# f64 weights by byte planes: two word shifts and a sign step replaced by two bf16 products

## The chip, the cores and the metric

The kernel runs on one core of a Trainium2 chip. Its engines are TensorE (PE: matmul; PEld: its weight loads), VectorE (DVE), ScalarE (ACT), GpSimd (POOL) and SyncE (SP), each with an instruction stream of its own that it works through in order; 16 DMA engines move data between HBM and SBUF. The metric is the device time of one execution, in microseconds; the median of 3 runs counts. Line numbers of the profile (L368) are lines of the kernel file. Nearly all of the first phase has the line L368, because a recorder collects the instructions and issues them from that line in an order that it plans; there the names of the tiles tell instructions apart.

## The reference

Three stages are computed, one after another:

```python
S_re, S_im = a*S (complex) + k x v          # gated recurrence over 768 steps, 4 x 8 heads of 48
y[:, :, t] = einsum(q[:, :, t], S_re)       # attention output
x = y as 3072 tokens x 384
h = max(x @ w1, x @ w2, x @ w3)             # 384 -> 768; the three weights and w_out are float64
x = (h @ w_out)                             # 768 -> 384
expert = argmax(softmax(cos(x, emb) / tau)) # one of 8 experts for each token
out = gate * (relu(x @ W1[e]) @ W2[e])      # 384 -> 1024 -> 384, float32 weights
```

The weights `w1`, `w2`, `w3` and `w_out` come as 8-byte floats. The host passes their bytes on as they are; the kernel makes float32 of them. This conversion is what the change is about.

## The kernel before

Phase 1 works on 12 units of 256 time steps (3 units for each of 4 batches). For each unit DVE and ACT prepare the complex decay (`front`: normalise; `mid`: running products; `back`: products with q and k into the tile `QK`), a DMA lays `QK` out by heads into a tile `S`, and TensorE does the attention of the unit's two halves (`attn`: transposes `pk`, scores `pa`, masked by DVE into `at`, state `pT`, output `py`), then the first MoE layer (`moe1`: products `ph` with `w1` and `w3`, maximum on DVE, products `px` with `w_out`). Float32 products are made of halves: a tile `xhi` that TensorE takes in one pass and a remainder `xlo`, and the same for weights (`whi`, `wlo`). Phase 2 sorts tokens by expert and runs the experts; its instructions stand in program order and are untouched by the change.

`weights` runs once, at the start of phase 1, and its products are needed by the first `ph`. It goes through 24 tiles of 128 x 384 f64 numbers: 6 of `w2` transposed (`w2t`), 12 of `w1` and `w3` (`w123`, loaded to tiles `r`), 6 of `w_out` (`wo`). POOL issues one DMA for each. Before the change a tile is converted so: ACT scales the upper word, read as float32, by 2^-112 (`f`), which shifts its exponent; the sign is set apart (for three tiles in four by two ACT instructions, Sign and a scaled Copy, for the fourth by one DVE mask); DVE shifts `f` left by 3 and puts the sign in, and a second DVE instruction shifts the lower word right by 29 and puts it in. A `w123` tile then goes on to TensorE: two passes with the identity bring it to a PSUM tile `pd`, products with `minus` subtract the `w2t` part, ACT copies `pd` out as `w` hi, TensorE subtracts that, ACT copies the rest out as lo. A `wo` tile is transposed (`pwt`), copied (`wt`) and multiplied with the expert embedding (`pG`); when all six are there, DVE copies `pG` into `wo`, and TensorE makes `pw` of `wo` and `w2t`. `pd`, `pwt`, `pw` and `ph` share three PSUM buffers with the tag "h".

The order of the instructions is made by a planner (`Recorder`): a list schedule with costs for each instruction, run forward and backward, in which each instruction has a key (unit number plus an offset of its stage) and a small bias by its kind (table `BIAS`). Where the plan leaves TensorE idle, `keep_warm` puts in short products with the identity (line 627). The order on each engine is fixed at build time; at run time an engine waits for semaphores.

Of the kernel before, what the change touches and what calls it, by code (L numbers as in the profile page):

```python
# [12 lines left out]
I32 = mybir.dt.int32  # L13
U32 = mybir.dt.uint32
# [109 lines left out]
class Recorder:  # L124
# [88 lines left out]
    def access(self, op, ap, write):  # L213
# [10 lines left out]
        else:  # L224
            idx = np.array([f])
# [3 lines left out]
            bits = np.zeros(pitch, np.uint8)  # L229
# [98 lines left out]
    def issue(self):  # L328
# [30 lines left out]
        for i in seq:  # L359
# [12 lines left out]
    BIAS = {"Cts": -0.91, "Cv": 0.78, "Gs": -0.3, "QKrv": -1.34, "QKs": -0.19, "Sg": 1.22, "Ss": 0.13, "Xg": 1.31,  # L372
            "Xs": -0.15, "cvhs": -1.13, "embv": -0.21, "enTv": -1.28, "end_s": -0.07, "fms": 1.79, "hhi_s": 0.15,
            "hlo_v": -0.8, "nrmss": 0.99, "nrmsv": -1.69, "pa_t": -0.95, "posv": 0.62, "pwtt": -1.99, "px__s": -1.23,
            "px__t": 0.63, "pyt": -0.99, "scv": 0.33, "w_s": 0.43, "wts": 1.11, "xhis": -1.08}
# [7 lines left out]
class Prog:  # L383
# [6 lines left out]
    def consts(self, pool):  # L390
# [22 lines left out]
        self.tiny = pool.tile([128, 1], F32, name="tiny")  # L413
        nc.gpsimd.memset(self.tiny, 1e-38)
# [294 lines left out]
    def weights(self, split=True):  # L709
# [45 lines left out]
        for k, (src, m, i, c) in enumerate(todo):  # L755
# [6 lines left out]
            raw = raw.rearrange("p (n w) -> p n w", w=2)  # L762
            f, sg = hs[k % 5], part(7 + k % 3).bitcast(I32)
            h = f.bitcast(I32)
            with self.keyed(-4 + k * 0.01):
                if split and k == self.AHEAD[0]:
                    self.load_a(1, q.gpsimd)
                if split and k == self.AHEAD[1]:
                    self.load_qk(0, q.gpsimd)
                q.gpsimd.dma_start(raw, src.bitcast(I32).rearrange("p (n w) -> p n w", w=2))  # L770
            if split and k % self.SIGNS:

                s.activation(sg.bitcast(F32), raw[:, :, 1].bitcast(F32), AF.Sign, bias=self.tiny)
                s.activation(sg, sg.bitcast(F32), AF.Copy, scale=2.0 ** 30, bias=-2.0 ** 30)
            else:
                v.tensor_scalar(sg, raw[:, :, 1], -0x80000000, None, op0=ALU.bitwise_and)
            s.activation(f, raw[:, :, 1].bitcast(F32), AF.Copy, scale=2.0 ** -112)
            v.scalar_tensor_tensor(h, h, 3, sg, op0=ALU.logical_shift_left, op1=ALU.bitwise_or)
            o = self.wo[:, i, :DM] if m is None else f if split and c is not None else w2t[:, i] if split else \
                self.w[:, m, i, c:c + n]  # L780
            v.scalar_tensor_tensor(o.bitcast(I32), raw[:, :, 0], 29, h, op0=ALU.logical_shift_right, op1=ALU.bitwise_or)
            if split and c is not None:
                both = self.tl(self.mw, [128, 2, n], f"w{m}{i}{c}", 1, f"w_{m}{i}{c}", F32R)
                self.whi[m, i, c // n], self.wlo[m, i, c // n] = both[:, 0], both[:, 1]
                pd = self.tl(self.pf, [128, n], "h", 3, f"pd{k}")
# [366 lines left out]
    SIGNS = 4  # L1152
# [634 lines left out]
```

## Time and profile before

| | |
|---|---|
| median of 3 runs | 778.13 us (777.83 to 778.33) |
| the profiled execution | 777.83 us, its span 775.9 us |
| TensorE busy | 719.6 us, 93% of the span |
| VectorE busy | 607.1 us, 78% |
| ScalarE busy | 441.5 us, 57% |
| mean granted TensorE clock | 0.983 of full speed |

The span is what the trace covers; 1.9 us of the execution lie outside it. Phase 1 reaches to about 513 us, phase 2 from there to the end. A busy time of an instruction includes its start-up, which overlaps with the one before it on the same engine; the distance of two starts is what an instruction costs in a full stream. In the names, numbers of buffers are left out.

### The profile page before, as it was taken

Reading aid. Unit: us, or ns where it says so; the run is one execution under the profiler, and the core shown is the slowest. Engines: PE = TensorE matmul, PEld = TensorE weight load, DVE = VectorE, ACT = ScalarE, POOL = GpSimd, SP = SyncE. Lnnn points to the kernel's source line nnn. Section 1 sums busy time; section 2 is a strip of 40 time slices with the busy share of each in tenths; the row PEclk is TensorE's granted clock in tenths of the full one; section 3 lists DMA queues with packets and bytes.
Section 4 is the critical chain, followed back from the end, with each engine's and each line's share of the span. In section 5 each row is a group of like instructions: output and inputs, shape, how many; then the busy total and the mean of one; then the engine's idle time right before and its main releaser. Section 6 shows DMA issues by size and latency. Waiting matters only on the chain. (4 is left out here: it accounts for less than half of the span.)

```text
span 775.9 us, 18425 instructions
## 1 busy us (share of the span) xinstructions
PE 719.6 (93%) x7318; PEld 657.1 (85%) x7318; DVE 607.1 (78%) x1211; ACT 441.5 (57%) x1007; POOL 104.6 (13%) x156
## 2 busy tenths in 40 slices
PE   0568989999999999999999999999999999999995
PEld 0447679899899989888998988989989898999985
DVE  8999799999999999999999722869986455546420
ACT  8997485656667555757455442167535466544521
POOL 6301000000000000000000000022122223324211
PEclk9987899999999999999999999999999999999999
DMA  8608062635345380834516240051058775691500
GB/s 330 263 21 197 1 174 69 139 131 137 106 105 119 91 209 13 197 99 119 137 37 140 60 86 22 13 233 42 22 236 335 283 299 213 210 368 49 186 22 26
DMA packets 28753, 107.42 MB, mean 138 GB/s; under 512 B 5061, under 2 KB 8180, under 8 KB 25569
## 3 DMA queue, kind: packets, MB, share of 16 engines
q1 hardware_dynamic: 20432, 77.55, 33.5%
q0 software_dynamic: 7952, 28.21, 11.3%
q8 instruction: 59, 0.97, 0.5%
q10 hardware_dynamic: 272, 0.39, 0.1%
q14 instruction: 38, 0.30, 0.1%
HBM read 96.35 MB, written 10.62 MB: 138 GB/s over the span
## 5 line engine op out<-in xcount | busy, mean ns | idle before, releaser
L368 PE MATMUL ph<-xhi,w 128*128 128x256 f32 x864 | 134.0, 291 | 0.9 <-ACT xhi L368 0.9
L368 PEld LDWEIGHTS ph<-xhi,w 128*128 128x128 f32 x864 | 114.3, 191 | 8.3 <-issue 4.7
L1298 DVE TENSOR_TENSOR w2l<-queue_q_buf,w2h 128x768 fp32r<-128x768 f32 x52 | 47.9, 954 | 39.1 <-ACT w2h L1297 39.0
L1336 PE MATMUL ph<-xh,w1s 128*128 128x256 f32 x264 | 77.0, 292 | 0.0
L368 PE MATMUL ph<-xlo,w 128*128 128x256 f32 x432 | 75.3, 283 | 0.4 <-DVE xlo L368 0.4
L1336 PE MATMUL ph<-xh,w1l 128*128 128x256 f32 x264 | 74.6, 283 | 0.0
L1336 PE MATMUL ph<-xl,w1s 128*128 128x256 f32 x264 | 74.6, 283 | 0.0
L1352 PE MATMUL py<-w2h,hlo 128*128 128x384 f32 x200 | 67.9, 340 | 1.8 <-DVE hlo L1341 1.8
L1352 PE MATMUL py<-w2h,hhi 128*128 128x384 f32 x200 | 69.1, 345 | 0.0
L1352 PE MATMUL py<-w2l,hhi 128*128 128x384 f32 x200 | 67.6, 338 | 0.0
L368 PEld LDWEIGHTS ph<-xlo,w 128*128 128x128 f32 x432 | 62.0, 191 | 0.6 <-DVE xlo L368 0.6
L368 POOL DMA_DIRECT2D v<-v x24 | 12.9, 538 | 365.4 <-PE py L368 364.5
L1341 DVE SCALAR_TENSOR_TENSOR hlo<-ph,hhi 128x512 fp32r<-128x512 f32 x50 | 34.3, 688 | 30.0 <-ACT hhi L1340 30.0
L1340 ACT ACTIVATE hhi<-ph 128x512 fp32r<-128x512 f32 x50 | 29.9, 598 | 49.0 <-PE ph L1336 48.8
L368 PE MATMUL pa<-S 112*128 112x128 f32 x384 | 51.7, 279 | 2.2 <-DVE at L368 1.7
L1336 PEld LDWEIGHTS ph<-xh,w1s 128*128 128x128 f32 x264 | 50.5, 191 | 3.8 <-issue 3.1
L368 PEld LDWEIGHTS pa<-S 112*128 112x128 f32 x384 | 48.2, 193 | 4.5 <-DVE at L368 2.9
L1297 ACT CAST w2h<-queue_q_buf 128x768 fp32r x52 | 40.8, 833 | 18.1 <-PE py L1352 16.7
L1336 PEld LDWEIGHTS ph<-xh,w1l 128*128 128x128 f32 x264 | 50.5, 191 | 0.5
L1336 PEld LDWEIGHTS ph<-xl,w1s 128*128 128x128 f32 x264 | 50.5, 191 | 0.0
L368 DVE TENSOR_TENSOR sa<-X 128x384 f32<-128x384 f32 x84 | 46.5, 554 | 0.7
L1292 DVE TENSOR_TENSOR w1l<-queue_q_buf,w1s 128x1536 fp32r<-128x1536 f32 x22 | 38.6, 1759 | 9.3 <-PE ph L1336 7.4
(399 smaller groups left out, 1809.1 us busy)
## 6 DMA issues: line engine op xcount, KB each, us to landing
queue_q_buf<-w SPq DMA_DIRECT2D x26, 1536.0 KB
S<-QK SPq DMA_DIRECT2D x46, 289.1 KB
X<-a SPq DMA_DIRECT2D x11, 768.0 KB
QKr<-qk SPq DMA_DIRECT2D x11, 768.0 KB
w1m<-w SPq DMA_DIRECT2D x5, 1536.0 KB
w2m<-w SPq DMA_DIRECT2D x5, 1536.0 KB
v<-v POOLq DMA_DIRECT2D x24, 224.0 KB, 3.6
r<-w POOLq DMA_DIRECT2D x12, 384.0 KB, 8.4
```

What stands on the lines that cost most here:

```text
L368: getattr(getattr(self.nc, c[0]), c[1])(*c[2], **c[3])
L1292: v.tensor_sub(wl[k], av.rearrange("p (a b) -> p a b", b=FF2)[:, :, c], w1[k].bitcast(F32))
L1297: s.copy(hi, b[:, c])
L1298: v.tensor_sub(lo, bv[:, c], hi.bitcast(F32))
L1336: t.matmul(ph[:, f], a, b, start=o == 0, stop=o == len(ops) - 1)
L1340: s.activation(hi, ph, AF.Relu).ins,
L1341: v.scalar_tensor_tensor(lo, ph, 0.0, hi.bitcast(F32), op0=ALU.max, op1=ALU.subtract).ins]
L1352: t.matmul(py, a[:, f, r], c[:, k % 4], start=o == 0, stop=o == 3 * KF - 1)
```

## The change

A double has its sign and the upper exponent bits in byte 7, and the rest of what a float32 needs in bytes 3 to 6. The new code loads the tile from byte 3 on (3069 bytes of each row of 3072, as bytes), so that bytes 3 to 6 of each number are one aligned word (`words`) and byte 7 is a small signed integer behind it (`top`). ACT makes relu(top + 72) as bf16, DVE makes top limited to -56..56 as bf16, and TensorE adds the first and subtracts the second in PSUM by two products with plus and minus identity (`sgn`, bf16): the sum is a small integer that holds sign and exponent. ACT scales it by 2^27, less a constant, into an integer word, and one DVE instruction shifts `words` right by 5 and puts that word in. For a `w123` tile the PSUM tile of these products is the `pd` that the later products use; the other tiles take one of the "h" buffers for it too. The sign by masks goes, with `SIGNS` and the constant `tiny`. The recorder's `access` now counts bytes in place of elements when it looks for overlaps, and the table `BIAS` has other values.

```diff
@@ -11,6 +11,7 @@
 F32R = mybir.dt.float32r
 BF16 = mybir.dt.bfloat16
 I32 = mybir.dt.int32
+I8 = mybir.dt.int8
 U32 = mybir.dt.uint32
 AF = mybir.ActivationFunctionType
 ALU = mybir.AluOpType
@@ -222,11 +223,12 @@
         elif ap.space == bass.MemoryType.DRAM:
             mask, p1 = -1, p0 + rows
         else:
-            idx = np.array([f])
+            idx, size = np.array([f]), mybir.dt.size(ap.dtype)
             for step, num in ap.ap[1:]:
                 if step:
                     idx = (idx[:, None] + step * np.arange(num)).reshape(-1)
-            bits = np.zeros(pitch, np.uint8)
+            idx = (idx[:, None] * size + np.arange(size)).reshape(-1)
+            bits = np.zeros(pitch * size, np.uint8)
             bits[idx] = 1
             mask, p1 = int.from_bytes(np.packbits(bits).tobytes(), "big"), p0 + rows
         new = (op, mask, p0, p1)
@@ -369,10 +371,8 @@
         return max(end)
 
     ENGINES = "vector", "scalar", "tensor", "gpsimd", "sync"
-    BIAS = {"Cts": -0.91, "Cv": 0.78, "Gs": -0.3, "QKrv": -1.34, "QKs": -0.19, "Sg": 1.22, "Ss": 0.13, "Xg": 1.31,
...
+    BIAS = {"M_s": -0.7, "QKv": 0.22, "Xg": -1.01, "Xv": -0.66, "enTv": -1.56, "fys": -0.19, "nrmsv": -0.29,
+            "rawxg": -1.19, "rg": 0.06, "sqxev": -0.1, "wtv": -0.72}
     PASSES, WAIT, LANES = 4, 130.0, 8
     START = {"vector": 1600.0, "gpsimd": 2200.0, "scalar": 2500.0, "sync": 1000.0}
     WINDOW = 4096 / 1.2
@@ -410,8 +410,11 @@
         idn = self.ident
         self.one = pool.tile([128, 1], F32, name="one")
         self.ln40 = pool.tile([128, 1], F32, name="ln40")
-        self.tiny = pool.tile([128, 1], F32, name="tiny")
-        nc.gpsimd.memset(self.tiny, 1e-38)
+        self.p72 = pool.tile([128, 1], F32, name="p72")
+        nc.gpsimd.memset(self.p72, 72.0)
+        self.sgn = pool.tile([128, 2, 128], BF16, name="sgn")
+        nc.scalar.copy(self.sgn[:, 0], self.ident)
+        nc.scalar.activation(self.sgn[:, 1], self.ident, AF.Copy, scale=-1.0)
         self.hln40 = pool.tile([128, 1], F32, name="hln40")
         nc.gpsimd.memset(self.one, 1.0)
         nc.gpsimd.memset(self.ln40, 40 * math.log(2))
@@ -759,30 +762,30 @@
             else:
                 raw = raws[ring if ring < 6 else 2 + ring % 4]
                 ring += 1
-            raw = raw.rearrange("p (n w) -> p n w", w=2)
+            row = raw.bitcast(I8)
+            words, top = raw[:, ::2], row[:, 4::8]
             f, sg = hs[k % 5], part(7 + k % 3).bitcast(I32)
-            h = f.bitcast(I32)
             with self.keyed(-4 + k * 0.01):
                 if split and k == self.AHEAD[0]:
                     self.load_a(1, q.gpsimd)
                 if split and k == self.AHEAD[1]:
                     self.load_qk(0, q.gpsimd)
-                q.gpsimd.dma_start(raw, src.bitcast(I32).rearrange("p (n w) -> p n w", w=2))
-            if split and k % self.SIGNS:
-
-                s.activation(sg.bitcast(F32), raw[:, :, 1].bitcast(F32), AF.Sign, bias=self.tiny)
-                s.activation(sg, sg.bitcast(F32), AF.Copy, scale=2.0 ** 30, bias=-2.0 ** 30)
-            else:
-                v.tensor_scalar(sg, raw[:, :, 1], -0x80000000, None, op0=ALU.bitwise_and)
-            s.activation(f, raw[:, :, 1].bitcast(F32), AF.Copy, scale=2.0 ** -112)
-            v.scalar_tensor_tensor(h, h, 3, sg, op0=ALU.logical_shift_left, op1=ALU.bitwise_or)
+                q.gpsimd.dma_start(row[:, :8 * n - 3], src.bitcast(I8)[:, 3:])
             o = self.wo[:, i, :DM] if m is None else f if split and c is not None else w2t[:, i] if split else \
                 self.w[:, m, i, c:c + n]
-            v.scalar_tensor_tensor(o.bitcast(I32), raw[:, :, 0], 29, h, op0=ALU.logical_shift_right, op1=ALU.bitwise_or)
+            both = f.bitcast(BF16)
+            up, mid = both[:, :n], both[:, n:]
+            s.activation(up, top, AF.Relu, bias=self.p72)
+            v.tensor_scalar(mid, top, -56.0, 56.0, op0=ALU.max, op1=ALU.min)
+            pd = self.tl(self.pf, [128, n], "h", 3, f"pd{k}")
+            with q.group() if split else ExitStack():
+                for x, j in ((up, 0), (mid, 1)):
+                    t.matmul(pd, self.sgn[:, j], x, start=j == 0, stop=j == 1)
+            s.activation(sg, pd, AF.Copy, scale=2.0 ** 27, bias=-72 * 2.0 ** 27)
+            v.scalar_tensor_tensor(o.bitcast(I32), words, 5, sg, op0=ALU.logical_shift_right, op1=ALU.bitwise_or)
             if split and c is not None:
                 both = self.tl(self.mw, [128, 2, n], f"w{m}{i}{c}", 1, f"w_{m}{i}{c}", F32R)
                 self.whi[m, i, c // n], self.wlo[m, i, c // n] = both[:, 0], both[:, 1]
-                pd = self.tl(self.pf, [128, n], "h", 3, f"pd{k}")
                 with q.group():
                     t.matmul(pd, self.ident, f, start=True, stop=True)
                     for b in range(3):
@@ -1149,7 +1152,6 @@
     SPLIT = 2
     BOTH = 1
     AHEAD = 3, 8
-    SIGNS = 4
     TAIL = 12000.0
     KEYS = {"conv": -0.9, "moe": 0.3, "mid": -1.0, "attn": -2.0, "back": -1.0, "front": -0.9, "early": 10.5, "max": 0.3}
```

The order changes on all engines. The numbers behind names are buffer numbers.

TensorE before, at its start: the first `w123` tiles go through `pd`; `cvh` and `S` hold the converted tile.

```order
L368 MATMUL pen<-ident,emb 128x8 x3
L627 MATMUL pd_169<-ident 128x128 x4
L368 MATMUL pd_169<-S_145,ident 128x384
L368 MATMUL pd_169<-minus,w2t 128x128 x3
L627 MATMUL pd_172<-ident 128x128 x2
L368 MATMUL pd_172<-S_145,ident 128x384
L368 MATMUL pd_172<-minus,w2t 128x128 x3
L368 MATMUL pd_176<-cvh_156,ident 128x384
L368 MATMUL pd_176<-minus,w2t 128x128 x3
L368 MATMUL pd_169<-w_168,minus 128x384
```

TensorE of the change, the first three `w123` tiles: the pair with `sgn` for the third of them, then the passes of all three.

```order
L370 MATMUL pd_184<-cvh_159,sgn 128x384
L370 LDWEIGHTS sgn
L370 MATMUL pd_184<-cvh_159,sgn 128x384
L370 MATMUL pd_177<-S_148,ident 128x384
L370 MATMUL pd_177<-minus,w2t 128x128 x3
L370 MATMUL pd_180<-S_148,ident 128x384
L370 MATMUL pd_180<-minus,w2t 128x128 x3
L370 MATMUL pd_184<-cvh_159,ident 128x384
L370 MATMUL pd_184<-minus,w2t 128x128 x3
L370 MATMUL pd_177<-w_178,minus 128x384
L370 MATMUL pd_180<-w_181,minus 128x384
L370 MATMUL pd_184<-w_185,minus 128x384
```

Each PSUM buffer is now taken two products earlier, and the tile passes ACT and DVE between the pair and the passes; TensorE's first instruction is no longer `pen` but such a pair for a `w2t` tile.

TensorE before, where the last `wo` tile has been turned: from the last `pG` to the third `pw`.

```order
L368 MATMUL pG<-enT,wt_216 128x8 x3
L368 MATMUL pa_1_254<-S_144 128x128 x4
L368 MATMUL pw_217<-wo,w2t 128x392 x6
L368 MATMUL pk_0_248<-ident,S_144 128x112 x4
L368 MATMUL pw_218<-wo,w2t 128x392 x6
L368 MATMUL pa_0_252<-S_144 128x128 x4
L368 MATMUL pk_0_261<-ident,S_144 128x112 x4
L368 MATMUL pw_219<-wo,w2t 128x392 x6
```

The same place of the change: `py_271` is the output of the first unit's first half.

```order
L370 MATMUL py_271<-xhi_273,unit 128x384
L370 MATMUL pG<-enT,wt_228 128x8
L370 MATMUL pG<-enT,wt_231 128x8 x3
L370 MATMUL pk_1_278<-ident,S_147 128x112 x4
L370 MATMUL pa_0_280<-S_147 128x128 x4
L370 MATMUL pa_1_282<-S_147 128x128 x4
L370 MATMUL pw_232<-wo,w2t 128x392 x6
```

The attention of the first unit's first half now stands ahead of the last `pG`; before it stood between and behind the `pw`.

DVE before, at the last masked scores (`at_1_337`) of the second unit.

```order
L368 SCALAR_TENSOR_TENSOR rr_380<-rr_380 128x768
L368 TENSOR_TENSOR at_0_335<-pa_0_334,mask 128x512
L368 TENSOR_TENSOR sb<-X_316 128x48
L368 TENSOR_TENSOR QK_381<-QKr_315,X_246 128x6x256
L368 TENSOR_TENSOR at_1_337<-pa_1_336,mask 128x512
L368 TENSOR_TENSOR Ct<-sb 128x24
```

DVE of the change at the same scores (`at_1_352`).

```order
L370 TENSOR_TENSOR at_0_350<-pa_0_349,mask 128x512
L370 TENSOR_TENSOR sa<-X_331 128x384
L370 SCALAR_TENSOR_TENSOR rr_395<-rr_395,QKr_330 128x768
L370 TENSOR_TENSOR X_331<-sa 128x2x96
L370 TENSOR_TENSOR QK_396<-rr_395,X_261 128x6x128
L370 TENSOR_TENSOR sa<-X_331 128x384
L370 TENSOR_TENSOR at_1_352<-pa_1_351,mask 128x512
```

Up to this row the change has 24 SCALAR_TENSOR_TENSOR of 128x384 fewer and 18 TENSOR_SCALAR of 128x384 more; of the third unit's preparation (`rr`, `QK`) more stands ahead of it, of the fourth unit's (`sa`, `X`) less.

## Rows read from the trace of the kernel before

**Rows 1.** The page: busy tenths of two engines in 40 slices of 19.4 us.
```profile
PE   0568989999999999999999999999999999999995
...
DVE  8999799999999999999999722869986455546420
```

**Rows 2.** Windows: busy us of each engine, TensorE's granted clock, DMA share, GB/s.
```profile
50.00:55.00 5.00, 2.16 (x13) 1.45 (x11) 5.00 (x10) 5.00 (x11) 0.00 (x0) 1.00 0.02 3
70.00:75.00 5.00, 4.81 (x23) 4.57 (x23) 4.90 (x18) 4.63 (x9) 0.04 (x1) 0.52 0.80 155
200.00:300.00 100.00, 99.27 (x1260) 91.38 (x1262) 96.72 (x193) 61.52 (x163) 2.68 (x5) 1.00 0.49 120
```

**Rows 3.** Waits of TensorE: who ended them, us in total, times, longest.
```profile
PE pen L368 <- DVE sb L368: 26.1, 1, 26.1
PE pd L368 <- ACT w L368: 9.4, 7, 2.1
```

**Rows 4.** Timeline of DVE: start, us, engine, line, operation, out<-in, shapes, [idle before].
```profile
31.63 0.54 DVE L368 SCALAR_TENSOR_TENSOR cvh<-r,cvh 128x384 int32<-128x384 int32 x1
32.10 0.23 DVE L368 TENSOR_TENSOR sb<-Ct,X 128x48 f32<-128x48 f32 x1
...
40.96 0.34 DVE L368 TENSOR_SCALAR S<-r 128x384 int32<-128x384 int32 x1
41.23 0.94 DVE L368 TENSOR_TENSOR m<-X,C 128x768 f32<-128x768 f32 x1
```

**Rows 5.** Timeline of ACT, 34 to 38 us.
```profile
34.13 0.53 ACT L368 ACTIVATE S<-S 128x384 int32<-128x384 f32 x1
34.54 0.56 ACT L368 ACTIVATE cvh<-r 128x384 f32<-128x384 f32 x1
35.00 0.55 ACT L368 ACTIVATE S<-r 128x384 f32<-128x384 f32 x1
...
36.62 0.84 ACT L368 CAST w<-pd 128x384 fp32r<-128x384 f32 x2
37.35 0.65 ACT L368 ACTIVATE S<-r,tiny 128x384 f32<-128x384 f32 x1
37.91 0.47 ACT L368 CAST w<-pd 128x384 fp32r<-128x384 f32 x1
```

**Rows 6.** Timeline of TensorE: weight and state products, the first MoE product, 384-column products.
```profile
92.06 4.13 PE L368 MATMUL pw<-wo,w2t 128*128 128x392 f32 x12
96.12 0.88 PE L368 MATMUL pT<-v,kt 128*32 128x48 f32 x64
...
107.17 0.97 PE L368 MATMUL ph<-xhi,w 128*128 128x256 f32 x6 [0.92 <-ACT xhi L368]
...
525.26 0.34 PE L1352 MATMUL py<-w2h,hlo 128*128 128x384 f32 x1
525.44 0.33 PE L1352 MATMUL py<-w2h,hhi 128*128 128x384 f32 x1
```

**Rows 7.** Timeline of DVE: idle times between 75 and 90 us.
```profile
79.45 0.21 DVE L368 COPY wo<-pG 128x48 f32<-128x48 f32 x1 [2.05 <-PE pG L368]
81.36 0.69 DVE L368 TENSOR_TENSOR at<-pa,mask 128x512 f32<-128x512 f32 x1 [0.53 <-PE pa L368]
87.76 0.96 DVE L368 TENSOR_TENSOR m<-X,C 128x768 f32<-128x768 f32 x1 [0.93 <-ACT C L368]
```

**Rows 8.** Timeline of DVE and TensorE: the second unit's last masked products.
```profile
137.08 0.68 DVE L368 TENSOR_TENSOR at<-pa,mask 128x512 f32<-128x512 f32 x1
...
135.16 2.80 PE L368 MATMUL px<-wo,h 128*128 128x392 f32 x8
...
139.47 1.05 PE L368 MATMUL py<-at,v 128*32 128x128 f32 x32
```

**Rows 9.** Timeline of POOL: two neighbouring loads of f64 weight tiles.
```profile
12.02 0.54 POOL L368 DMA_DIRECT2D r<-w  x1 [0.44 <-DMA r<-w]
12.99 0.54 POOL L368 DMA_DIRECT2D r<-w  x1 [0.44 <-DMA S<-w2t]
```

More of the change, by code (lines that the diff above doesn't have):

```diff
@@ L371 @@
     ENGINES = "vector", "scalar", "tensor", "gpsimd", "sync"
-    BIAS = {"Cts": -0.91, "Cv": 0.78, "Gs": -0.3, "QKrv": -1.34, "QKs": -0.19, "Sg": 1.22, "Ss": 0.13, "Xg": 1.31,
-            "Xs": -0.15, "cvhs": -1.13, "embv": -0.21, "enTv": -1.28, "end_s": -0.07, "fms": 1.79, "hhi_s": 0.15,
-            "hlo_v": -0.8, "nrmss": 0.99, "nrmsv": -1.69, "pa_t": -0.95, "posv": 0.62, "pwtt": -1.99, "px__s": -1.23,
-            "px__t": 0.63, "pyt": -0.99, "scv": 0.33, "w_s": 0.43, "wts": 1.11, "xhis": -1.08}
+    BIAS = {"M_s": -0.7, "QKv": 0.22, "Xg": -1.01, "Xv": -0.66, "enTv": -1.56, "fys": -0.19, "nrmsv": -0.29,
+            "rawxg": -1.19, "rg": 0.06, "sqxev": -0.1, "wtv": -0.72}
     PASSES, WAIT, LANES = 4, 130.0, 8
```

## The prediction

> **What bounds the kernel now.** I read the page's slices first. TensorE shows 9 in nearly every slice from the sixth on, and low digits in the first five; VectorE shows 9 up to the twenty-second [rows 1]. So the end is set by how early TensorE gets into its full stream. The windows say the same with numbers: from 200 to 300 us TensorE is busy 99.27 of 100 us and VectorE 96.72, while at 50 to 55 us VectorE and ScalarE are both busy 5.00 of 5 and TensorE 2.16 [rows 2]. The list of waits names what TensorE lacks there: 26.1 us for its first instruction, then 9.4 us in seven waits for ScalarE's copies of converted weights [rows 3]. The first MoE product starts at 107.17 us [rows 6], and behind it there is hardly any idle time. Time saved in the head is thus time saved at the end, if the stream behind it is fed as well as before; and VectorE, which feeds it, is as full as TensorE.
>
> **The change part by part.** Costs in a full stream are distances of starts.
>
> VectorE: a two-input instruction of 384 numbers takes 0.47 (31.63 to 32.10), a one-input one 0.27 (40.96 to 41.23) [rows 4]. Removed: 24 of the two shifts for each of 24 tiles, one remains, so 24 x 0.47 = 11.3, and 6 masks x 0.27 = 1.6. Added: 24 limits of `top` x 0.27 = 6.5. Net 6.4 us less. The trace has no one-input instruction that reads single bytes. From above it is bounded by the two-input price, 0.47, which leaves 12.9 - 11.3 = 1.6 us of gain; from below by half of 0.27, if a narrower type goes twice as fast, which gives 12.9 - 3.2 = 9.7. I take 0.27: the mask that it is nearest to reads every second word, the same eight-byte distance, and the count of numbers is equal. The Trainium skill ("VectorE: DVE Perf Modes", section "What auto-detection actually checks") lets a one-source instruction between SBUF operands take two numbers a cycle whatever their width. By that rule the price is the mask's 0.27 and the gain 6.4; without it, at the two-input price, 1.6. The 0.27 row agrees for 4-byte numbers; no row here shows bytes.
>
> ScalarE: removed are 18 pairs of Sign (0.56, 37.35 to 37.91) and scaled Copy (0.41, 34.13 to 34.54), and 24 scalings (0.46, 34.54 to 35.00) [rows 5]: 18 x 0.97 + 24 x 0.46 = 28.5. Added are 24 Relu with a bias from a tile, at the Sign's price, and 24 copies out of PSUM at 0.37 (two take 36.62 to 37.35): 24 x 0.93 = 22.3. Net 6.2 less, so ScalarE does not become the one that holds VectorE up; the two `sgn` copies at the very start stand before its first data.
>
> TensorE: added are 48 products of 384 columns. Two such products lie 0.18 apart at the full clock [rows 6], so 8.6 us, at the half clock twice that, 17.3. From below they cannot cost less than nothing. I put them at nothing on the path: the first dozen fall into the 26.1 us in which TensorE has had no work, the rest into the 9.4 us and the gaps of the 5-us window that shows 2.16 busy [rows 2, 3]. If that cover were gone, the 8.6 to 17.3 us would come on top.
>
> Loads: 24 as before, 0.97 us apart on the queue [rows 9], each with rows of 3069 in place of 3072 bytes, from an odd address. I take no difference; bounds stand with the fifth rival.
>
> The order: two things move. The first unit's attention stands before the last `pG`, so less lies between the finished weights and the first MoE product. And at the second unit's last masked scores, VectorE has 24 two-input and adds 18 one-input instructions less and more in front: 24 x 0.47 - 18 x 0.27 = 6.4 us earlier; what else moved across that row adds up to 0.1. TensorE has 3.7 us less to do between the first MoE product and this place: the `px<-wo,h` group of 2.80 us [rows 8] and the state product now come behind. So where VectorE sets this place, the end moves by 6.4 - 3.7 + 1.7 = 4.4 us (before, the scores were done at 137.76 and used only at 139.47, which is the 1.7 [rows 8]). To this comes what VectorE loses no more: its idle times of 2.05, 0.53 and 0.93 while TensorE and ScalarE were late with `pG`, `pa` and `C` [rows 7], 3.5 us, which the new order can give back in full or not at all. That is 4.4 to 7.9. I take 6.4, the plain VectorE sum, near the middle.
>
> Sum: 777.8 (the profiled execution, 775.9 of span and 1.9 around it) - 6.4 = 771.4. The median of the runs is 778.1, 0.3 higher; I leave the forecast at 771.4.
>
> **The rivals.**
>
> 1. TensorE's early start leads. Before, 27.5 us lay between the end of VectorE's copy of `pG` (79.66) and the first MoE product at 107.17 [rows 6, 7]. Now only the three `pw` (4.13 each), the second half's state and output products (0.88 and twice 1.05), and two short groups lie there, for the unit's state and the remainders of `pw`, taken at 0.88 each [rows 6, 8]: 17.1. In front of the last `wo` tile VectorE has 6.4 us of conversion less and 5.0 more of other work (the first scores, the third unit's normalising), so the copy comes 1.4 earlier, the first MoE product 11.8, and the time is 766.0, if VectorE keeps up. Against it: VectorE has no slack to keep up with.
>
> 2. Slower: the three "h" buffers. A `w123` tile now holds its buffer for the pair, ScalarE's copy and VectorE's shift as well: 0.64 at half clock + 0.37 + 0.47, and two hand-overs of, say, 0.7, an estimate by a third of the longest wait of 2.1 [rows 3]: 2.9 us. Twelve tiles in threes are four rounds: 11.6 us if nothing covers it. 777.8 - 6.4 + 11.6 = 783.0. It decides from 1.6 us a round, where it eats the 6.4. For it speaks that ScalarE was already what TensorE waited for; against it, that the pairs of the first rounds can run in TensorE's idle start.
>
> 3. The byte read runs at the two-input price: 24 x 0.20 = 4.8 us come back: 776.2.
>
> 4. The conversion was hidden by loads and TensorE's weight chain: at 70 to 75 us TensorE is busy 4.81 of 5 at a granted clock of 0.52 [rows 2], the lower level of 1.2 GHz, after a gap. If this half-speed stretch still ends the head, nothing is gained: 777.8.
>
> 5. The odd address halves the loads' rate: 24 x 0.97 = 23.3 us more until the last is in, at about 51 us in place of 28; the weights that are converted last would then be some 7 us late: 778.4. The Trainium skill ("DMA: Bandwidth & Descriptors", section "How a descriptor splits into AXI transactions") cuts a descriptor at 256-byte boundaries: bytes 3 to 3071 make 12 pieces, as many as 0 to 3071. By that rule this rival has no chance and the forecast stays. No row here has an odd address.
>
> That the change does not do what it says I leave out of the chances: the instructions are there in the order.
>
> **How the numbers follow.** Forecast 0.52 (own range 769.9 to 773.4, from 7.9 and 4.4), first rival 0.12, second 0.12, third 0.10, fourth 0.08, fifth 0.06. A range of 766.0 to 781.0 reaches to the first rival and well into the second, and leaves out about 0.15. About 0.2% (1.6 us) is what can be told from no change: faster means below 776.6, slower above 779.7. Faster: 0.50 of the forecast, all of the first rival, 0.08 of the third, 0.02 of the others: 0.72. Within: 0.15, from the fourth and fifth and the edges. Slower: 0.13, the second and a piece of the fifth.
>
> **What would show it.** In the changed profile: the one-input instruction on bytes with about 0.34 busy (0.54 would be rival 3); ScalarE's Relu near 0.64 and its copy from PSUM near 0.48; TensorE's first pair before 15 us; the first MoE product between 95 and 101 us; VectorE's last masked scores of the second unit ending near 130; TensorE again over 99% busy from 200 to 300 us. I am wrong if ScalarE or VectorE shows new idle times for `pd` in the head of more than 6 us together, if loads land later than the queue's 0.97 spacing, or if TensorE idles for `at` or `S` between 100 and 160 us by more than 4 us.

## The result and the profile after

The changed kernel took 786.64 us (median of 5 executions, 784.21 to 787.68), the kernel before beside it 778.33 (777.83 to 779.86): ratio 1.0086, interval 1.0062 to 1.0110. The forecast was 771.4. The profiled execution took 784.48 us with a span of 782.7, so 6.8 us of span over the one before.

The slices of the changed kernel's page (19.6 us each), which answer to [rows 1]: TensorE starts earlier than before, but its fourth slice goes with PEclk 6, and a 7 stands in the twenty-seventh, where the row before had nothing under 8 between the third and the last.

```profile
PE   1677998999999999999999999979998999999995
...
DVE  8996999999999999999999713859995455646420
...
PEclk9996999999999999999999999999999999999998
```

The window that answers to the last of [rows 2] (busy us of TensorE, its weight loads, VectorE, ScalarE, POOL; granted clock; DMA share; GB/s): at 200 to 300 us TensorE is busy 98.08 us, not over 99. From 50 to 55 us it is busy 3.39 of 5, more than before.

```profile
200.00:300.00 100.00, 98.08 (x1273) 89.94 (x1274) 96.35 (x189) 62.98 (x171) 3.76 (x7) 1.00 0.52 124
```

TensorE's waits up to the experts (who ended them; us, times, longest), beside [rows 3]. The first instruction now comes after 14.6 us in place of 26.1, and the waits for converted weights (`w`) have sunk from 9.4 to 2.8. In their place stand a second item of 4.8 for the embedding, 4.2 more behind ScalarE's `S`, and waits for `h` and `kt`.

```profile
PE pd L370 <- ACT S L370: 18.8, 4, 14.6
PE pen L370 <- DVE Ct L370: 4.8, 1, 4.8
PE px L370 <- DVE h L370: 3.4, 3, 1.7
...
PE pd L370 <- ACT w L370: 2.8, 6, 0.8
...
PE pa L370 <- ACT kt L370: 2.5, 1, 2.5
```

The prices came out as forecast. All engines from 63 us on (start, busy, engine, tiles, shapes, in brackets the idle time before and what ended it):

```profile
63.15 0.84 ACT L370 ACTIVATE fy<-X 128x768 f32<-128x768 f32 x1 [3.98 <-DMA X<-a]
...
64.00 0.47 ACT L370 ACTIVATE S<-pd 128x384 int32<-128x384 f32 x1
64.37 0.85 ACT L370 CAST w<-pd 128x384 fp32r<-128x384 f32 x2
64.50 0.56 DVE L370 SCALAR_TENSOR_TENSOR wo<-S 128x384 int32<-128x384 int32 x1 [2.99 <-ACT S L370]
64.52 0.80 PE L370 MATMUL pd<-cvh,sgn 128*128 128x384 bf16 x2 [3.71 <-ACT S L370]
...
64.97 0.35 DVE L370 TENSOR_SCALAR S<-rawxhi 128x384 bf16<-128x384 int8 x1
...
65.24 0.35 DVE L370 TENSOR_TENSOR X<-sa 128x192 f32<-128x192 f32 x1
```

VectorE's limit on bytes is busy 0.35, and the next instruction starts 0.27 later (64.97 to 65.24): the price of the sum, next to [rows 4]. ScalarE's copy out of PSUM takes 0.37 of the stream (64.00 to 64.37). But the rows show something else too. ScalarE stands 3.98 us, until 63.15, before the square `fy<-X` of the third unit: it waits for the load of that X. Behind it on ScalarE is the copy `S<-pd`, which frees the "h" buffer that TensorE's next pair needs (3.71 us of idle time, to 64.52) and makes the word for VectorE's `wo` (2.99 us, to 64.50). All three engines stand still at once. On SyncE's queue the load was issued at 54.60, and directly behind it stand five transfers of `QK` (five more were on POOL's queue); 8.5 us passed until ScalarE could go on. That they slow the load is argued from the queue and was not tried, and the kernel before speaks against it as the whole reason: there the same load was issued at 61.48 with the same ten transfers right behind it, and ScalarE used it at 66.87, after 5.4 us, without a wait for it. In the run with the stall put in (below) it was 6.2 us, from 51.52 to 57.67. What made it 8.5 stays open.

```profile
54.60 0.33 SPq L370 DMA_DIRECT2D X<-a  x1
54.98 4.03 SPq L370 DMA_DIRECT2D S<-QK  x5
```

Behind this gap the granted clock falls. Windows of the changed kernel:

```profile
60.00:65.00 5.00, 1.29 (x8) 0.62 (x7) 1.94 (x5) 1.85 (x5) 0.00 (x0) 0.83 1.05 209
65.00:70.00 5.00, 3.87 (x15) 2.73 (x15) 4.72 (x17) 4.78 (x11) 1.19 (x2) 0.50 0.76 184
70.00:75.00 5.00, 5.00 (x26) 5.00 (x25) 3.46 (x8) 3.40 (x9) 0.00 (x0) 0.50 0.12 47
75.00:80.00 5.00, 5.00 (x38) 4.58 (x36) 3.11 (x14) 3.30 (x7) 0.00 (x0) 0.81 0.02 3
```

From 65 to 75 us TensorE runs at 0.50 of full speed, the level of 1.2 GHz; from 70 us on it is full while VectorE is busy 3.46 and 3.11 of 5. VectorE's longest wait there is for TensorE's scores:

```profile
75.94 0.69 DVE L370 TENSOR_TENSOR at<-pa,mask 128x512 f32<-128x512 f32 x1 [2.43 <-PE pa L370]
```

VectorE's idle time from 60 to 80 us adds up to 6.8 us (20 less 1.94, 4.72, 3.46 and 3.11). In the kernel before it was 2.6 in the same stretch:

```profile
60.00:80.00 20.00, 16.87 (x96) 15.34 (x96) 17.38 (x50) 15.01 (x33) 3.83 (x7) 0.76 0.80 189
```

So VectorE waits 4.2 us more in this stretch, of the 6.4 us that it was spared; over the first 90 us it is 3.5 more (11.1 against 7.6, from the windows over whole stages below). The marks of the forecast, in the changed kernel: the first pair, the first MoE product, the second unit's output product, the first product of the experts; then VectorE's last copy of `pG` into `wo`, and its last masked scores.

```profile
14.57 0.80 PE L370 MATMUL pd<-S,sgn 128*128 128x384 bf16 x2 [14.57 <-ACT S L370]
...
102.62 0.88 PE L370 MATMUL ph<-xhi,w 128*128 128x256 f32 x6
...
136.04 1.05 PE L370 MATMUL py<-at,v 128*32 128x128 f32 x32
...
515.92 0.49 PE L370 MATMUL pxg<-ident,xg 128*128 128x128 f32 x3
```

```profile
86.00 0.20 DVE L370 COPY wo<-pG 128x48 f32<-128x48 f32 x1
...
134.36 0.68 DVE L370 TENSOR_TENSOR at<-pa,mask 128x512 f32<-128x512 f32 x1
```

The first MoE product is 4.55 us earlier than in [rows 6], the output product 3.43 earlier than in [rows 8], and yet the experts begin 3.84 later than before:

```profile
512.08 0.49 PE L368 MATMUL pxg<-ident,xg 128*128 128x128 f32 x3
```

Marks of the order had moved; the end had not followed. Windows over whole stages, before and after:

```profile
0.00:90.00 90.00, 52.12 (x231) 40.94 (x232) 82.39 (x199) 72.03 (x174) 23.09 (x73) 0.89 0.53 175
90.00:140.00 50.00, 47.29 (x720) 40.30 (x722) 48.70 (x97) 30.38 (x80) 1.66 (x3) 1.00 0.37 94
140.00:512.08 372.08, 368.28 (x4501) 339.17 (x4494) 322.41 (x655) 204.77 (x550) 15.32 (x24) 1.00 0.45 110
```

```profile
0.00:90.00 90.00, 57.94 (x373) 41.11 (x374) 78.89 (x198) 69.00 (x169) 24.08 (x74) 0.92 0.55 178
90.00:140.00 50.00, 44.51 (x603) 37.51 (x602) 49.15 (x90) 30.96 (x81) 1.61 (x3) 0.97 0.45 116
140.00:515.92 375.92, 369.39 (x4485) 340.34 (x4484) 321.61 (x655) 201.29 (x544) 14.79 (x23) 1.00 0.43 105
```

Busy time does not tell how much work is done, since a product at the lower clock is busy for longer, and the new pairs are in it; so count the products instead. Without the pairs and the short products of `keep_warm`, the changed kernel had issued 24 `ph<-xhi,w`, 12 `ph<-xlo,w` and 6 `pa<-S` more than the one before by 120 us, 4 to 5 us of TensorE's time (an estimate: six `ph` take 0.72, from 102.62 to 103.34). By 140 us the lead was gone: 12 `py<-at,v` more and 3 `px<-wo,h` fewer, all else alike. Before and after, from 120 to 140 us:

```profile
120.00:140.00 20.00, 19.39 (x348) 17.26 (x350) 19.86 (x37) 9.90 (x24) 0.54 (x1) 1.00 0.09 30
```

```profile
120.00:140.00 20.00, 15.56 (x314) 13.65 (x314) 19.74 (x31) 11.95 (x29) 1.07 (x2) 0.91 0.30 83
```

TensorE stands idle there 4.4 us against 0.6, and from 130 to 135 us the granted clock is 0.66. Its longest wait is for the copy `kt`. The transposes that it copies (`pk`, 126.41) were done at 127.01, but on ScalarE the copy stood behind two steps on `rr` and a square `fy<-X` for later units, and came at 128.96:

```profile
128.96 0.51 ACT L370 COPY kt<-pk 128x448 f32<-128x448 f32 x1
```

```profile
129.52 1.16 PE L370 MATMUL pa<-S 112*128 112x128 f32 x8 [2.50 <-ACT kt L370]
```

From 140 us to the experts the changed kernel needs 3.8 us more (375.92 against 372.08), of which 2.7 are idle time of TensorE (6.5 against 3.8), and the experts' stage is 3.0 us longer (266.78 against 263.82). So the stall at 61 us alone does not explain the loss against the kernel before: after it the changed kernel was still ahead. The lead went from 120 to 140 us, and the end fell behind after that.

### The profile page after: what moved, and what is told of

It is laid out like the page before. It is cut to its first block, busy times and chain, and to the rows that moved or that the text cites. A ratio compares the mean times of both kernels' runs of the same rounds, so it can differ in the third digit from the quotient of the medians.

```text
span 782.7 us, 18446 instructions
## 1 busy us (share of the span) xinstructions
PE 723.3 (92%) x7334; PEld 655.6 (84%) x7334; DVE 605.4 (77%) x1205; ACT 436.1 (56%) x997; POOL 103.6 (13%) x156
## 5 line engine op out<-in xcount | busy, mean ns | idle before, releaser
L370 DVE TENSOR_TENSOR at<-pa,mask 128x512 f32<-128x512 f32 x48 | 32.8, 687 | 18.6 <-PE pa L370 18.4
```

The lines of the kernel that those rows point to most:

```text
L370: getattr(getattr(self.nc, c[0]), c[1])(*c[2], **c[3])
```

## The experiments

In the expectations theory 1 is that the 48 new products are paid in full on TensorE, theory 2 that the order of instructions which came with the change holds waits that cost the time. Theory 3, from the ninth run on, is that the stretches at half clock behind TensorE's gaps are what the order costs. (The run without products names a third theory of its own, the hand-overs.) "Order held" means that the planner works with unchanged costs, and instructions are doubled, left out or moved only when they are issued, so that everything else stays where it was.

**More and fewer products, order held.** Edits, one for each run:

```diff
 with q.group(): two matmuls into pd, plus `up`, minus `mid`
+    q.cur.calls *= 2                        # e1_four
+    del q.cur.calls[1:]                     # e2_one, with the copy's scale 2^24 and a bias to match
+    q.skip.append(q.cur)                    # e3_none: not issued, copy reads `up`
```

> The changed kernel with its order of instructions held, and each pair of sgn products issued twice over (the second pair overwrites the first): 48 more products of 384 columns, nothing else. Theory 1 (TensorE's work): the 48 products of the change are paid in full, at 0.18 us each at the full clock, so 48 more add 8.6 us or more to the changed kernel's 786.6: about 795. Theory 2 (the order): the loss comes from waits that the new order holds (60.95 to 64.5, 117 to 140 and 490 to 519 us), and TensorE has idle time in the conversion; 48 more products then add under 3 us: at most 789.

> The changed kernel with its order held, and one product in place of two for each tile: only the plus product of `up`, with the copy's scale and bias chosen so that weights of 2^-15 to 2 come out as before (smaller ones come out a little wrong, so this is no version to keep). The limit on VectorE stays, its result is not used. 24 products less. Theory 1: 4.3 us or more less than 786.6, about 782. Theory 2: within 1.5 us of 786.6.

> The changed kernel with its order held, and no sgn product: ScalarE's copy reads `up` from SBUF in place of the product from PSUM (weights under 2^-15 a little wrong, as with one product). VectorE and ScalarE keep their instructions; 48 products and the two hand-overs VectorE to TensorE to ScalarE are gone. Theory 1: 8.6 to 17 us less than 786.6, 770 to 778. Theory 2: 784 to 787, the waits stay. A third theory (the hand-overs): TensorE's waits of 18.8 us for ScalarE's S go but for the first 14.6, so about 4 us less, 782; it parts from theory 1 by the run with one product, where the hand-overs stay and the time would not move.

Four products a tile: 786.33 us (778.43 to 790.23), one: 783.82 (783.03 to 787.14). Against before that is 1.0083 (1.0050 to 1.0116) and 1.0078 (1.0062 to 1.0095), with 1.0086 for two. The three can't be told apart: theory 1 is out. The run without products came to 1021.65 us and can't be compared as a whole: in the held order the Relu of a later tile in the same buffer writes `up` before the copy reads it, so weights come out changed, and the experts' stage is another one (507 us long). Its first phase can be read, since its instructions do not depend on the data: the experts begin at 512.74, where two profiles of the changed kernel have 515.92 and 514.93. That is 2.2 to 3.2 us earlier, nearer to the 4 of the hand-overs than to the 8.6 of theory 1.

**The stall at 61 us taken away, order held otherwise.**

```diff
 start, end, _, seq = plan
+for i, j in (512, 272), (511, 536), (509, 290), (510, 509):
+    seq.remove(i)
+    seq.insert(seq.index(j) + 1, i)     # ScalarE's squares of X, VectorE's product, ScalarE's next step
```

> The changed kernel with its order held but for four instructions of the third unit's normalising: ScalarE's two squares of X, which wait 3.98 us for the load of X at 59.2 us with copies of finished products queued behind them, go behind five such copies and a Relu; VectorE's product and ScalarE's next step follow. Theory 2: the stall of all three engines at 61 to 64.5 us goes, and 3 to 4 us with it: about 783. Theory 1: TensorE is short of work there, not of time; the 3.7 us that it stands idle return as far as it is full behind, also about 783, but the gap of 117 to 140 us grows by what comes early: between 783 and 786.6. At 786 or above the stall at 61 us is not on the path at all.

783.55 us, 1.0055 (1.0034 to 1.0076): 3.1 under the 786.64 of the first comparison, but level with the 783.70 that the unchanged copy gave later (e12_after_again), so this run does not decide. The gap at 61 us is gone in its profile (TensorE 3.92 of 5 at 60 to 65 us), and the half-clock stretch is there all the same:

```profile
60.00:65.00 5.00, 3.92 (x23) 2.62 (x21) 4.79 (x12) 2.88 (x8) 0.00 (x0) 1.00 1.04 243
...
70.00:75.00 5.00, 5.00 (x26) 5.00 (x26) 4.65 (x13) 4.49 (x10) 0.00 (x0) 0.50 0.18 69
```

**The table of planner offsets exchanged.** The edit is the table `BIAS` alone.

```diff
-BIAS = {own table}
+BIAS = {}                 # e5_after_plain, e6_before_plain
+BIAS = {the other's}      # e7_after_oldtable, e8_before_newtable
```

> The changed kernel with an empty table of planner offsets (BIAS), so the order is the planner's own. With the next run it shows the conversion alone, without either table. Theory 1 (TensorE's work): slower than the old conversion with an empty table by 4 to 9 us. Theory 2 (the order): the difference is that of VectorE's relief, 4 to 8 us less than the old conversion, or it has no fixed sign.

> The kernel before with an empty table of offsets. Both theories: slower than 778.3, since its table was made for it; theory 2 expects the distance to 778.3 to be as large as the loss of the change or larger (8 us), theory 1 less (under 4).

> The changed kernel with the table of offsets of the kernel before. Theory 1: 4 to 9 us above the kernel before, 782 to 787, as with its own table. Theory 2: could come out anywhere from 772 to 795; the spread over the three tables (own, empty, old) is 5 us or more.

> The kernel before with the table of offsets of the changed kernel. Theory 1: 4 to 9 us under the changed kernel's 786.6, as the conversion is the only thing that differs. Theory 2: no fixed sign; near or above 786.6 if this table makes the poor order.

| table | old conversion | new conversion |
|---|---|---|
| old | 777.78 | 773.22, ratio 0.9942 (0.9927 to 0.9956) |
| empty | 783.22, 1.0074 (1.0049 to 1.0099) | 783.54, 1.0087 (1.0066 to 1.0108) |
| new | 786.62, 1.0108 (1.0092 to 1.0124) | 786.64, 1.0086 (1.0062 to 1.0110) |

This decides between theories 1 and 2. With one and the same table the new conversion is not measurably slower (with the empty and the new table the intervals overlap); with the old one it gains 4.6 us (773.22 against 777.78), and this version beats both kernels. The gain shows under that table alone, so it belongs to the two together. The new table costs the changed kernel 13.4 us against the old one (11.2 by the ratios) and the old conversion 8.8. The table sets the order and, through the plan, how many short products `keep_warm` puts in: 8 in the changed kernel, 40 with the old table. These are hardly the reason, since a version with 24 is as fast (773.65, the run e16_old_newloads below). In the version with the old table the marks are those of the forecast (95 to 101, near 130):

```profile
97.05 0.88 PE L370 MATMUL ph<-xhi,w 128*128 128x256 f32 x6
...
505.58 0.49 PE L370 MATMUL pxg<-ident,xg 128*128 128x128 f32 x3
```

```profile
129.00 0.69 DVE L370 TENSOR_TENSOR at<-pa,mask 128x512 f32<-128x512 f32 x1
```

No stall stands at 61 us, the granted clock is 1.00 in every 5-us window up to the experts (on the first 30 us see the last section), and VectorE is idle 0.6 us from 60 to 80:

```profile
60.00:80.00 20.00, 18.51 (x227) 15.62 (x226) 19.45 (x54) 17.65 (x41) 2.19 (x4) 1.00 0.42 92
```

**TensorE kept busy in its gaps, order held.**

```diff
 start, end, _, seq = plan
+self.ops[253].calls *= 10     # e9_fill, e10_fill2: the pair before the stall at 61 us
+self.ops[612].calls *= 6      # e10_fill2: the transposes before the gap at 127 us
```

> The changed kernel with its order held; the one sgn pair that TensorE issues just before its stall at 61 us (pd18) is issued ten times in place of once, 18 useless products of 0.18 us. ScalarE and VectorE stall as before (they wait for the load of X); only TensorE is busy from 60.9 to about 63.8 in place of idle. Theory 3 (the clock): the gap of 3.71 us is what the granted clock falls to 0.50 for from 65 to about 78 us; without it the clock stays at 1.00 there, and the slices of 60 to 80 us give back the 6.8 us that they lost: 780. Theory 2 (waits alone): useless products change nothing: 786.6, and the clock behind the stall is beside the point. Theory 1 (TensorE's work): 786.6 to 790.

> As the run before, and the four transposes in front of the gap of 2.50 us at 127 us (pk3_0) are issued six times. Theory 3: the slice of 130 to 135 us, at 0.66, also goes back to 1.00, which gives 1.7 us more: 778. Theory 2: 786.6. Theory 1: 787 to 791.

> The changed kernel itself once more, beside the three. All theories: 786.6 within 2 us, with the granted clock at 0.50 behind a gap of TensorE near 61 us.

The copy itself gave 783.70 (780.38 to 785.24), 1.0061 (1.0038 to 1.0085), 2.9 under the first comparison, where 2 was expected at most; so the changed kernel stands 5 to 8 us over the one before. The fillings gave 788.00, 1.0139 (1.0110 to 1.0168), and 788.46, 1.0135 (1.0107 to 1.0162): worse. The filling was there (20 products in 3.41 us), and in the profiled execution the half-clock stretch shrank to a part of one window:

```profile
61.27 3.41 PE L371 MATMUL pd<-cvh,sgn 128*128 128x384 bf16 x20
```

```profile
60.00:65.00 5.00, 4.85 (x29) 3.14 (x30) 2.45 (x6) 1.07 (x3) 0.00 (x0) 1.00 1.06 197
...
70.00:75.00 5.00, 5.00 (x34) 4.79 (x33) 4.28 (x12) 4.24 (x10) 0.00 (x0) 0.66 0.28 85
```

In the profile of the second it came back behind a wait of 1.68 us at 70 us, and longer than before:

```profile
70.26 0.90 PE L372 MATMUL pwt<-ident,wo 128*128 128x128 f32 x3 [1.68 <-DVE wo L372]
```

```profile
70.00:75.00 5.00, 4.74 (x22) 4.34 (x23) 4.67 (x17) 3.93 (x9) 0.55 (x1) 0.50 0.36 133
...
80.00:85.00 5.00, 5.00 (x23) 4.56 (x24) 1.89 (x9) 1.93 (x5) 0.00 (x0) 0.50 0.00 0
```

In the profile of the first, other windows went lower than in the changed kernel: 0.69 at 45 to 50 us and 0.50 at 130 to 135, where it has 1.00 and 0.66. So theory 3 is refuted as a cure: filling this gap neither keeps the clock up for sure nor saves time. Why the fillings cost 4 to 5 us stays open. These runs do not show that time at the lower clock costs nothing, since they did not raise the clock: its mean is 0.972 to 0.984 in the executions of the first filling and 0.983 to 0.987 in those of the copy.

**The new conversion in the good order.** The old table, order held; one edit in each run.

```diff
 v.tensor_scalar(mid, top, -56.0, 56.0, op0=ALU.max, op1=ALU.min)
+q.ops[-1].calls *= 2                     # e13_old_limit2
 with q.group(): two matmuls
+    del q.cur.calls[1:]                  # e11_old_one, copy as in e2_one
 start, end, _, seq = plan
+seq.remove(510)                          # e14_old_stall: ScalarE's square of X
+seq.insert(seq.index(217) + 1, 510)
```

> The changed kernel with the old table of offsets (773.2), its order held, with one sgn product for each tile in place of two (weights under 2^-15 a little wrong). Theory 1: 24 products less on a TensorE that runs at the full clock throughout: 4.3 us less, 769. Theory 3: the products fill gaps; with half of them the gaps of 1.0 to 1.6 us at 42, 51 and 59 us get longer, and if the clock falls behind one of them the time is 2 to 7 us longer, 775 to 780; if it holds, 773. Theory 2: 773, within 1 us.

> The changed kernel with the old table (773.2), its order held, each of the 24 limits of `top` on VectorE issued twice. That is 24 x 0.27 = 6.5 us more for VectorE. If VectorE's time in the head reaches the end one to one, as the prediction's sum took it: 779.7. If TensorE's own chain sets the end in this order: 773 to 775. In between: VectorE is on the path for a part of the head only.

> The changed kernel with the old table, its order held but for one instruction: ScalarE's square of the third unit's X moves nine places forward, to about 54.2 us, where the load of X has not landed, with copies of products queued behind it. Theory 2 (waits): a stall of some 3 us, and the time is up by about as much, 776. Theory 3 (clock): the gap of TensorE also lets the granted clock fall to 0.50 for a stretch behind it, which this order did not show anywhere: up by 3 us and 3 to 6 more, 779 to 782. If the stall is absorbed behind: 773.

One product in place of two: 773.62, 0.9947 (0.9930 to 0.9965), level with 0.9942. So the products cost nothing measurable in this order either, in which the granted clock shows 1.00 throughout the first phase.

The limits twice: 785.88, 1.0082 (1.0061 to 1.0102), so 12.7 us over 773.22 for 6.5 us of VectorE. The first MoE product comes 11.55 later than 97.05:

```profile
108.60 0.88 PE L370 MATMUL ph<-xhi,w 128*128 128x256 f32 x6
```

By the two ratios to the kernel before it is 1.4% or 10.9 us. So VectorE's time in the head reaches the end. That the loss is larger than the 6.5 us goes together with a lower clock: the mean granted clock of these executions is 0.981 to 0.991, with the old table alone 0.992 to 0.997. The two parts were not separated.

The stall put in: 778.93, 1.0005 (0.9992 to 1.0018), 5.7 us over 773.22. ScalarE waits 3.60 us for the load, TensorE 4.49 behind it, and the clock is 0.66 in the next window; it recovers by 65 us.

```profile
57.67 0.84 ACT L372 ACTIVATE X<-X 128x768 f32<-128x768 f32 x1 [3.60 <-DMA X<-a]
```

```profile
59.54 0.44 PE L372 MATMUL pd<-w,minus 128*128 128x384 f32 x1 [4.49 <-ACT w L372]
```

```profile
60.00:65.00 5.00, 4.56 (x16) 2.84 (x16) 3.77 (x9) 3.84 (x10) 0.00 (x0) 0.66 0.59 109
65.00:70.00 5.00, 4.64 (x30) 3.31 (x28) 4.93 (x13) 4.96 (x11) 0.57 (x1) 1.00 0.00 0
```

A stall like the one at 61 us is thus worth about 5 us in a good order (4.9 by the ratios, 5.7 by the medians). Theory 2 had 3 us, the wait alone; 778.93 lies just under theory 3's 779 to 782, the wait and a stretch at the lower clock. So here the stretch behind the gap seems to cost as well.

**Which entries of the table.**

```diff
+new table, its entries Xg, rawxg, rg as in the old one    # e15_new_oldloads
+old table, its entries Xg, rawxg, rg as in the new one    # e16_old_newloads
+old table, the 14 entries for ScalarE alone               # e17_old_act
+old table, the other 14 alone                             # e18_old_rest
```

> The changed kernel with its own table, but the entries for loads on POOL's queue (Xg, rawxg, rg) as in the old table. If the order of the first loads is what costs (TensorE's gap of 4.83 us at 24 us, and what follows): near 773 to 777. If not: 782 to 787, as with its own table.

> The changed kernel with the old table, but the entries for loads on POOL's queue as in the new one. If the order of the first loads is what costs: 781 to 787. If not: 771 to 776.

> The changed kernel with those 14 entries of the old table that are for ScalarE (names ending in s), the other 14 left out. If the good order is that of ScalarE's copies and squares: 772 to 777. If it is not: 781 to 787, as with an empty table.

> The changed kernel with the 14 entries of the old table for the other engines, those for ScalarE left out. If the good order is that of ScalarE's instructions: 781 to 787. If it is that of VectorE, TensorE and the loads: 772 to 777. If both halves come out near 783, no half makes it, and each order is good or poor as a whole.

784.03, 1.0073 (1.0047 to 1.0100), and 773.65, 0.9943 (0.9926 to 0.9960): the order of the first loads is not the reason. The halves: ScalarE's entries 780.21, 1.0028 (0.9999 to 1.0057), the others 783.91, 1.0072 (1.0046 to 1.0097). Neither half makes the good order for sure. Which entries together make it stays open.

But the run with ScalarE's entries says something else: its twelve executions go from 774.40 us, at a mean granted clock of 0.995, to 785.66, at 0.981. One and the same order can thus come out as fast as the best version or nearly as slow as the changed kernel. With four products it is alike: 778.43 at 0.987 and 790.23 at 0.968. Hold this against the kernels. The one before has 0.979 to 0.985, the changed kernel 0.979 to 0.984 in the first comparison: its loss is not a matter of the mean clock. The new conversion with the old table has 0.992 to 0.997. If 0.014 go with 11 us, an estimate from the run with ScalarE's entries, then that difference in the clock alone could be worth the whole gain of 4.6 us. The runs do not show which of the two, the waits or the clock, is the cause of the other.

## Why the prediction was wrong

The step that failed is the one headed "The order". It counted which instructions stand in front of one mark, VectorE's last masked scores of the second unit, found 6.4 us less of them there, and let the end follow ("where VectorE sets this place, the end moves by 6.4 - 3.7 + 1.7"). Its bounds, 4.4 to 7.9, held only ways in which waits of the old order go; none in which the new order brings a wait of its own, although the change replaced the whole table of offsets. The exchange of tables shows that this replacement is worth 11 to 13 us in the changed kernel, over twice the 4.6 us that the conversion gains with the old table, and of the other sign. Of the rivals none named it. Its sign of a poor order was TensorE idle for `at` or `S` between 100 and 160 us by more than 4; there TensorE waited 1.1 us for `S` and none for `at`, but 2.5 for `kt` and 1.4 for `h`, which the sign did not cover.

- VectorE's price was right: 0.27 for the byte limit, so rival 3, the two-input price, is out. That its time in the head reaches the end is shown by the run with doubled limits, in the good order. The 773.22 with the old table lies near the forecast of 771.4, but this does not prove the sum of 6.4: that version also has the higher clock, which the prediction did not count, and part of the agreement may be luck.
- ScalarE's prices were right (0.37 for the copy). That it "does not become the one that holds VectorE up" was wrong in the new order: VectorE waits 2.99 us for `S` at 64.50, not for lack of ScalarE's time, but because ScalarE stands before a load.
- "I put them at nothing" for the 48 products was right: in the changed order by the runs with four and with one, in the good order by the run with one.
- The mark, the first MoE product, came at 102.62 in place of 95 to 101. With the old table it is 97.05.
- That the end follows the mark was wrong: 3.43 us earlier at the second unit's output product, 3.84 later at the experts. The prediction had seen that the `px<-wo,h` group now comes behind this mark; counted by products the two kernels are level at 140 us, and what follows is 3.8 us longer.
- Rival 1 took its lead from VectorE's copy of `pG`, which was to end 1.4 us earlier. It starts at 86.00, 6.6 us later than in [rows 7]. From its end to the first MoE product are 16.4 us, close to the rival's 17.1: the distance was right, the start was not.
- Rival 2 had the right place: the "h" buffers are what TensorE waits for at 64.52. But it priced four rounds at 2.9 us each; the trace has one such wait of 3.71, and its cause is ScalarE's wait for X. That its 783.0 lies near the result is no support for it.
- Rival 4 spoke of the half-clock stretch at 70 to 75 us. It is there in the kernel before, which has the old table, and in the changed kernel, and absent in the new conversion with the old table; so it goes neither with the table alone nor with the conversion alone. The one version that gains is the one without it. How much of the 4.6 us is this stretch and how much VectorE's time was not separated.
- Rival 5, the odd address: byte loads stand in the version that takes 773.22, so they do not cost what it feared; the page gives a median of 8.5 us from issue to landing for the loads of `r`, and 8.4 before.

What is shown: that the order which the new table makes costs the time, that the conversion with the same table does not, and that a stall of the kind seen at 61 us costs about 5 us when it is put into a good order. What is not shown: which waits make the loss in the changed kernel. Taking the stall at 61 us away gave between 0 and 3 us. Against the kernel before, the lead of 120 us goes in idle times of TensorE of 2.50 and 1.36 us that end at 129.5 and 138.4 us and in a stretch at the lower clock, and none of these was taken away alone. The experts' stage goes with the table too, though its own instructions are the same: it is 262.9 to 265.0 us long in six profiles with the old table and 266.0 to 268.6 in nine with the new one, with both conversions on either side and in each group one profile with exchanged load entries. Why stays open; at its start TensorE waits 2.8 us for ScalarE's `xT` in the changed kernel and 1.2 before.

## What to carry to other kernels

When a change also replaces the numbers that set the order, price the order as an item of its own with both signs, and time the code with the old numbers first: here this one run took 773.22 us, where the same code with its own table takes 786.64. An earlier mark is no earlier end; count how much work of the full engine has been done by then, not which instruction has been reached. In an in-order stream look at what is queued behind each wait for a load: a square that nobody needed yet held the copies that two other engines stood for. And when executions of one order differ by several us, look at the granted clock of each before reading a difference between orders.

## What the runs showed of the hardware

- 768 KB took 8.5 us from issue to use in the changed kernel and at most 5.4 in the one before, with ten small-grained transfers issued right behind it on two queues in both; over these spans the DMA share was 0.97 at 261 GB/s and 0.96 at 319.
- The granted clock does not follow from the length of the last gap alone. It went to 0.50 behind a gap of 3.71 us, and in another run behind one of 1.68; with the old table a gap of 2.74 us ending at 202.35 left it at 1.00. Useless products in one gap shortened the stretch in one profile and not in the other.
- A granted clock of 1.00 in the first 30 us of a profile is not the pace of the products. In the changed kernel a pair takes 0.80 us at 18.33, in a window with 1.00, as it does at 64.52, where the clock falls to 0.50; at 44.43 it takes 0.48. With the old table the pairs take 0.80 up to 29.14 and 0.48 at 34.46. So "1.00 throughout" holds from some 34 us on.

```profile
18.33 0.80 PE L370 MATMUL pd<-cvh,sgn 128*128 128x384 bf16 x2 [1.02 <-ACT cvh L370]
...
44.43 0.48 PE L370 MATMUL pd<-cvh,sgn 128*128 128x384 bf16 x2 [0.52 <-ACT w L370]
```

- 6.5 us more on VectorE cost 10.9 to 12.7 us at the end. TensorE at half clock in the same stretch of that run is a likely part of it (0.84 on the mean from 60 to 80 us), but this was not separated.
- Executions of one and the same order differ by 5 us (the unchanged copy: 780.38 to 785.24) to 12 (four products: 778.43 to 790.23), where those with the old table lie within 3.9. In the widest two orders the longest execution has the lowest mean granted clock (0.968 and 0.981) and the shortest the highest (0.987 and 0.995).
